# A delta-rule attention followed by two feed-forward layers: weight conversions one step earlier, chunk 1's attention pieces respaced

## The chip, the core and the metric

The kernel runs on one core of a Trainium2 chip. The metric is the device time of one launch in microseconds; the median of three runs is quoted, and one further execution was recorded by the profiler.

## What is computed

With B = 4, H = 8, S = 768, D = 48, all in float32:

```python
k_n = k / (norm(k) + 1e-6)
for t in range(S):                       # per batch and head, state is D x D
    y[t] = q[t] @ state
    v_old = k_n[t] @ state
    state = state + beta[t] * outer(k_n[t], v[t] - v_old)
x = y as [3072 tokens, 384]
x = relu(x @ w_in) ** 2 @ w_out          # 384 -> 2048 -> 384
out = max(x @ w1, x @ w2, x @ w3) @ w3out  # 384 -> 768 -> 384
```

The weights arrive as 64-bit words and are turned into float32 on the chip.

## The kernel before

**Chunks.** The sequence is cut into 12 chunks of 64 tokens. Within a chunk the recurrence becomes a triangular system. Its 64x64 inverse per head is built from two 32x32 inverses and one merging block. The 32x32 inverses of two chunks are computed together by `solve32` on VectorE: a preparation (`prep`, with the norms of the keys), 30 pairs of small operations (lines 290 and 292) and a last product (line 293), whose result goes to DRAM (`finish32`). The products of keys that it starts from, and the masked query-key products, come from `kkps`, which multiplies on TensorE, copies with ACT (line 204), masks with VectorE (line 205) and stores to DRAM from SP.

**Attention of a chunk** (`attention(c)`) is a generator whose pieces are: `load` (`load_x`: the inverses and a key block from DRAM), `st0` (v is scaled; pA and pY = keys and queries times the state Sb; v minus pA), `zz` (pZ, the merging block's first product, with the copy z and the transpose xT), `ww` (pW, written back into xb), `mm_u` (U = inverse times v, in pU; copied by line 480 or 482 to SBUF), `st2` (pY gets the masked products times u, pD the state's growth; Sb is added by line 505, yy copied out by lines 530 and 532) and `st3` (transposes pT, split into xh and xl). Heads go in two groups p = 0 and 1, called pairs below. pA, pZ, pW, pU, pD, pT and the norms' transpose pt share one PSUM tag "at" with two buffers.

U doesn't fit into one bank: units from n on go into spare columns of another bank. Pair 1 uses its own pY for two units (n = 6), pair 0 uses px, the bank of the second product, for four (n = 4); in chunk 2 both use pY.

**The first feed-forward layer of a chunk** (`moe_a`) has 8 products `s1` (18 matmuls of 256 columns into p1, of which there are two buffers; then ACT's Relu, Square and copy gh, and VectorE's gl) and 8 products `s2` (12 matmuls of 384 columns into px), two behind. Every number is split into a high part rounded to the matmul's format and a low part, so each product has three matmuls. At the end px is transposed to xs on VectorE (line 618) and stored.

**The order of the work** is written out by `steps` (line 633). It runs through the steps of `moe_a` of chunk c (16, or 32 halves in chunk 1) and behind each step takes from every other generator as many pieces as are due: a number is a rate per step, a list names the steps. In step order, the generators of `extra` come one after the other. During chunk c the attention of chunk c + 1 runs, and in odd chunks `kkps`, in even chunks the solve for the two chunks behind. Chunk 0 also has `weights`.

The program's order is a priority: a scheduler then places the instructions on each engine by simulated time. From chunk 1 on `pin` (line 263) chains TensorE's and VectorE's instructions, so that these two engines keep the order as written; in chunk 0 nothing is pinned, and ACT, POOL and SP never are. `behind(a, b)` orders a after b.

**Conversions.** A block of w_in or w_out is fetched by SP (line 93) into one of 16 raw buffers, 9 of them for the first blocks only. `turn` (line 101) then takes ACT's magnitude (104), VectorE's shift (107), two joins (111, 113), ACT's high part (115) and VectorE's low part (118). Four of the w_out blocks take two more ACT operations (125, 126) in place of VectorE's. Nine of the 32 blocks are turned ahead of chunk 0; `weights(3, 2)` (line 757) turns three in its first call and two in each of the ten others, and fetches the next. It orders the shifts behind the last but one gl that has been written (`after[:] = gls[-2:-1]`), and the next steps of the solve behind its last low part.

**Norms.** `norm(nm)` transposes the norms on TensorE (pt, line 282) and copies them to normT with four ACT copies (line 318). In `solve32` it is called for all groups but the first at pair 24 of the solve.

**Queues.** `load_x` issues on SP and ACT for chunk 0 and on POOL for all other chunks.

Of the kernel before, what the change touches and what calls it, by code (L numbers as in the profile page):

```python
# [35 lines left out]
HALVED = [(c, c + 1) for c in range(0, NC, 2)]  # L36
U2 = 2 * Q


def delta_moe(ctx, tc, kc, ab, kt, vt, beta, beta32, beta16, kq, w_in, w_out, w1, w2, w3, w_out2, out):  # L40
    nc = tc.nc
    vec, act, pool = nc.vector, nc.scalar, nc.gpsimd
# [151 lines left out]
    def kkps(cs, ps_, dma=nc.sync):  # L194

        todo = [(c, p) for c in cs for p in range(2)]
        ahead = len(kcts) - (len(kcts) < 4)
        for n in range(min(ahead, len(todo))):
            kkp_load(*todo[n], dma)
        for n, (c, p) in enumerate(todo):  # L200
            ks = kss[nk[1] % len(kss)]
            nk[1] += 1
            pk, pq = kk_matmul(c, p, ps_[n % len(ps_)])
            kk_ends[0] = act.copy(ks[:, 0], pk).ins
            kk_ends[1] = vec.tensor_mul(out=ks[:, 1], in0=pq, in1=mask.unsqueeze(1).broadcast_to([128, U2, C])).ins
            for i in mul_after:
                behind(kk_ends[1], i)
            yield
            kk_store(c, p, ks[:, 0], dma)

            for t in range(2):
                dma.dma_start(p_d[c][64 * t:64 * t + 64, U2 * p:U2 * p + U2], ks[64 - 64 * t:128 - 64 * t, 1])
            if n + ahead < len(todo):
                kkp_load(*todo[n + ahead], dma)
            yield
# [122 lines left out]
    def load_x(c):  # L338

        k21 = att.tile([128, B * Q, 32], F32, name="k21", tag="k21", bufs=1)  # L340
        x1 = att.tile([128, U2, 32], F32, name="x1", tag="x1", bufs=1)
        ds = []
        for t in range(2):
            if c:
                ds.append(pool.dma_start(k21[64 * t + 32:64 * t + 64], kk_d[c][32:64, t, :, 0:32]))
            for h in range(2):
                o, hs = 64 * t + 32 * h, slice(32 * h, 32 * h + 32)
                i = (pool if c else (nc.sync, act)[t]).dma_start(xb[o:o + 32, :, hs], xt_d[c][h, t].rearrange("u j i -> j u i"))
                if c:
                    ds.append(i)  # L350
                else:
                    x_loaded.append(i.ins)
        for t in range(2):
            for g in range(2):
                o = 64 * t + 32 * g
                i = (pool if c else (nc.sync, act)[t]).dma_start(x1[o:o + 32], xt_d[c][0, t, U2 * g:U2 * g + U2].rearrange("u j i -> j u i"))
                ds.append(i)
        for i in x_after:
            if c:
                for d in ds:  # L360
                    behind(d.ins, i)
        return k21, x1
# [25 lines left out]
    def attention(c):  # L388
# [68 lines left out]
        def mm_u(p):  # L457
            x, r = tiles[c, p][2], tiles[c, p][6]
            pU = ps_at.tile([128, U2, D], F32, name="pU", tag="at")
            own = p or c == 2  # L460
            n = U2 - (0 if not c else 2 if own else 4)
            if c:
                free = pYs[p] if own else pxs
                over = free[0].rearrange("p (b n) -> p b n", b=1) if own else free[0]
                over = over[:, :, DM:DM + 2 * D].rearrange("p b (u d) -> p b u d", d=D)
            order = [u for i in range(U2) for u in (i, n + i) if (i < n if u == i else u < U2)]
            for u in order:
                for t in range(2):
                    if u < n:
                        pe.matmul(pU[half(t), u], x[half(t), u], r[half(t), u], start=True, stop=True)  # L470
                    else:
                        o = over[half(1 - t), (u - n) // 2, (u - n) % 2]
                        i = pe.matmul(o, x[half(t), u], r[half(t), u], start=False, stop=True, skip_group_check=True)
                        for j in free[1:]:
                            behind(i.ins, j)
            u_ = fresh("u", p, 7, [128, U2, D])
            on_vec = p and c != 1
            def put(to, po):
                if on_vec:
                    last_vec[0] = vec.tensor_copy(to, po).ins  # L480
                else:
                    last_act[0] = act.copy(to, po).ins
            put(u_[:, 0:n], pU[:, 0:n])
            if c:
                for m in range(n, U2, 2):
                    for t in range(2):
                        put(u_[half(t), m:m + 2], over[half(1 - t), (m - n) // 2])
# [214 lines left out]
    def part(g, n):  # L702
        for _ in range(n):
            next(g, None)
            yield
# [5 lines left out]
    if True:  # L711
# [19 lines left out]
        def solve32(g, load=(nc.sync, nc.sync), store=((nc.sync,) * 2,) * 2, landing=0):  # L731
            M, a, ready, norm = start32(g, load)
            for _ in range(landing):
                yield
            if landing:
                prep_after[:] = last_gl
            nm = ready()
            if not g:
                normed.append(norm(nm))
            yield  # L740
            for n, i in enumerate(solve(vec, M, 32, 64 * len(HALVED[g]), a, tmp32)):
                for j in solve_after:
                    behind(i.ins, j)
                ops.append(i.ins)
                if g and n == 24:
                    norm(nm)
                yield
            finish32(g, M, store)

        def later(n, g):  # L750
            for _ in range(n):
                yield
            yield from g
# [3 lines left out]
        def weights(first, each):  # L757
            n = first
            while queue:
                if last_gl[0] and last_gl[0] not in gls:  # L760
                    gls.append(last_gl[0])
                after[:] = gls[-2:-1]
                words(n)
                n = each
                after.clear()
                prep_after[:] = solve_after[:] = parted[-1:]
                yield
# [136 lines left out]
        ahead_ = {}  # L904
        for c in range(NC):
            extra = []
            if c == 0:
                solve_next = solve32(1, (pool,) * 2)
                extra += [(1.0, weights(3, 2)), (11 / 15.0, later(3, attention(1))), (4.0, later(20, part(solve_next, 10)))]
            elif c == 1:  # L910
                pinned.update({first_matmul.ins.engine: None, last_gl[0].engine: None})
                first_solve = [0] * 3 + [1 + n * 13 // 20 for n in range(20)]
                extra += [(first_solve, solve_next), ([14, 16, 24, 25, 27, 29, 31], attention(2))]
                ahead_[2] = solve32(2, landing=1)
                extra += [([13, 14, 18, 19, 20, 21, 22, 23], kkps(HALVED[2], (at,))), ([26], ahead_[2], True)]
                solve_after[:] = last_vec
                prep_after.clear()
            elif c + 1 < NC:
                extra.append(([1, 2, 5 + c // 9, 7 + c // 9, 10, 12, 14] if c % 2 else [1, 2, 4, 6, 8, 11, 13], attention(c + 1)))
            if c == 2:  # L920
                kc_after.clear()
                solve_after.clear()
            if c in ahead_:
                extra.append(([1] * (c == 2) + [1 + (c == 2) + n * (14 - (c == 2)) // 32 for n in range(32)], ahead_[c]))
            if c > 1 and c in KK:
                extra.append(([3, 4, 4, 5, 6, 7, 8, 9], kkps(HALVED[KK[c]], (at,))))
                ahead_[c + 1] = solve32(KK[c], landing=1)
                extra.append(([11, 14], ahead_[c + 1], True))
            if c == 9:
                after[:] = last_gl  # L930
                load_w3s = w3load((0, 1))
            if 9 <= c < NC - 1:
                extra.append((0.4, part(load_w3s, 6)) if c > 9 else (0.8, later(6, part(load_w3s, 6))))
            if c == NC - 1:
                pr.close()
                wb = ctx.enter_context(tc.tile_pool(name="wb", bufs=1, side="right", reuse_waits="tile"))
                first = []
                extra.append((0.6, chain(load_w3s, w3load((2,)))))
                extra.append((0.5, later(2, x2_steps(0, wb, first))))
            steps(moe_a(c, gp, c == 1), *extra)  # L940
# [114 lines left out]
```

## Time and profile before

| | |
|---|---|
| median of 3 runs | 946.04 us (945.61 to 950.18) |
| the profiled execution's own time | 944.06 us |
| its span, first to last instruction | 942.3 us |
| TensorE busy (PE) | 875.7 us, 93% |
| VectorE busy (DVE) | 498.9 us, 53% |
| ACT busy | 391.6 us, 42% |
| GpSimd busy (POOL) | 150.9 us, 16% |
| mean granted TensorE clock | 0.954 of 2.4 GHz |

The profile names an engine's work by line, output and input tile. Busy times are sums over instructions; a busy TensorE isn't one at its peak. Where an engine stood still, the row says for how long and which instruction on which engine ended the wait ("issue": nothing that the profile shows). The granted clock is a share of 2.4 GHz; 0.50 is 1.2 GHz. Chunk 0's first product begins at 76.7 us of the span, chunk 1's at 142.2, chunk 2's at 196.7.

### The profile page before, as it was taken

Reading aid. Unit: us, or ns where it says so; the run is one execution under the profiler, and the core shown is the slowest. Engines: PE = TensorE matmul, PEld = TensorE weight load, DVE = VectorE, ACT = ScalarE, POOL = GpSimd, SP = SyncE. Lnnn points to the kernel's source line nnn. Section 1 sums busy time; section 2 is a strip of 40 time slices with the busy share of each in tenths; the row PEclk is TensorE's granted clock in tenths of the full one; section 3 lists DMA queues with packets and bytes.
Section 4 is the critical chain, followed back from the end, with each engine's and each line's share of the span. In section 5 each row is a group of like instructions: output and inputs, shape, how many; then the busy total and the mean of one; then the engine's idle time right before and its main releaser. Section 6 shows DMA issues by size and latency. Waiting matters only on the chain.

```text
span 942.3 us, 26555 instructions
## 1 busy us (share of the span) xinstructions
PE 875.7 (93%) x11422; PEld 848.9 (90%) x11422; DVE 498.9 (53%) x1118; ACT 391.6 (42%) x807; POOL 150.9 (16%) x245
## 2 busy tenths in 40 slices
PE   4448978998999999999999999999999999999998
PEld 4347868898999999999999999999999999999998
DVE  2987979169427843784388275577432323323221
ACT  1665774334344534453544466564221222212211
POOL 2252110331231124012311420002000000000000
PEclk8557979999999999999999999999999999999999
DMA  9987722762583267327621643234200101000000
GB/s 197 318 226 202 213 75 67 209 149 64 133 193 101 63 146 200 81 63 181 148 61 61 156 126 98 59 106 139 76 22 30 43 26 33 27 26 9 18 17 34
DMA packets 121125, 98.83 MB, mean 105 GB/s; under 512 B 75904, under 2 KB 101296, under 8 KB 121008
## 3 DMA queue, kind: packets, MB, share of 16 engines
q1 hardware_dynamic: 100224, 58.23, 24.3%
q0 software_dynamic: 11712, 32.41, 12.9%
q10 hardware_dynamic: 9072, 6.49, 2.4%
q8 instruction: 90, 1.47, 0.7%
q14 instruction: 27, 0.22, 0.1%
HBM read 72.45 MB, written 24.64 MB: 103 GB/s over the span
## 4 chain that ended last, share of the span: by engine, by line
PE 81%; DVE 7%; ACT 6%; DMA 4%; issue 2%; ACTq 0%; SPq 0%; DVEq 0%
PE p L963 24%; PE px L598 20%; PE p L578 19%; PE po L980 8%; DMA rawp<-in_moe_w_in_dram 2%; PE pU L470 2%; PE pY L520 1%; DVE gl L587 1%; PE pk L187 1%; DVE buf L290 1%; PE pA L451 1%; DVE buf L292 1%; DMA raw<-in_moe_w_out_dram 1%; PE pW L426 1%; PE pZ L417 1%
## 5 line engine op out<-in xcount | busy, mean ns | idle before, releaser
L963 PE MATMUL p<-x_h,w 128*128 128x384 f32 x864 | 220.1, 336 | 0.0
L598 PE MATMUL px<-wout,gh 128*128 128x384 f32 x768 | 204.7, 347 | 1.6 <-ACT wout L115 1.5
L578 PE MATMUL p<-xh,win_h 128*128 128x256 f32 x576 | 169.7, 295 | 2.4 <-DVE gl L587 0.9
L578 PE MATMUL p<-xl,win_h 128*128 128x256 f32 x576 | 163.9, 285 | 0.3 <-DVE xl L542 0.3
L578 PE MATMUL p<-xh,win_l 128*128 128x256 f32 x576 | 164.0, 285 | 0.0
L963 PEld LDWEIGHTS p<-x_h,w 128*128 128x128 f32 x864 | 156.1, 188 | 0.0
L587 DVE TENSOR_TENSOR gl<-p,gh 128x512 fp32r<-128x512 f32 x96 | 66.3, 690 | 154.5 <-ACT gh L586 154.3
L963 PE MATMUL p<-x_l,w 128*128 128x384 f32 x432 | 145.2, 336 | 0.0
L598 PEld LDWEIGHTS px<-wout,gh 128*128 128x128 f32 x768 | 138.7, 194 | 3.2 <-ACT wout L115 1.8
L584 ACT ACTIVATE p<-p 128x512 f32<-128x512 f32 x96 | 55.9, 582 | 187.8 <-PE p L578 186.7
L598 PE MATMUL px<-wout,gl 128*128 128x384 f32 x384 | 131.1, 341 | 0.0
L578 PEld LDWEIGHTS p<-xh,win_h 128*128 128x128 f32 x576 | 111.0, 193 | 6.0 <-DVE gl L587 1.4
L578 PEld LDWEIGHTS p<-xl,win_h 128*128 128x128 f32 x576 | 111.1, 193 | 0.8 <-DVE xl L542 0.7
L578 PEld LDWEIGHTS p<-xh,win_l 128*128 128x128 f32 x576 | 111.3, 193 | 0.0
L969 DVE TENSOR_TENSOR mx<-p,mx 128x384 f32<-128x384 f32 x48 | 26.7, 557 | 124.1 <-PE p L963 124.1
L963 PEld LDWEIGHTS p<-x_l,w 128*128 128x128 f32 x432 | 81.2, 188 | 0.0
L971 ACT CAST hh<-mx 128x384 fp32r<-128x384 f32 x48 | 24.6, 513 | 119.6 <-DVE mx L970 119.5
L598 PEld LDWEIGHTS px<-wout,gl 128*128 128x128 f32 x384 | 74.1, 193 | 0.0
L292 DVE TENSOR_TENSOR buf<-buf 128x30 f32<-128x30 f32 (+9 forms) x180 | 60.5, 336 | 6.0
L290 DVE TENSOR_TENSOR buf<-buf 128x30 f32<-128x30 f32 (+9 forms) x180 | 59.9, 333 | 4.8
L586 ACT CAST gh<-p 128x512 fp32r<-128x512 f32 x96 | 56.4, 588 | 2.5
L585 ACT ACTIVATE p<-p 128x512 f32<-128x512 f32 x96 | 56.0, 583 | 2.6
(183 smaller groups left out, 1341.9 us busy)
## 6 DMA issues: line engine op xcount, KB each, us to landing
kq<-in_kc_dram POOLq DMA_DIRECT2D x22, 448.0 KB, 5.5
raw<-in_moe_w_dram SPq DMA_DIRECT2D x18, 384.0 KB, 3.5
p<-p POOLq DMA_DIRECT2D x22, 256.0 KB, 3.9
raw<-in_moe_w_out_dram SPq DMA_DIRECT2D x13, 384.0 KB, 3.3
v<-in_vt_dram POOLq DMA_DIRECT2D x24, 192.0 KB, 3.4
ktp<-in_kt_dram POOLq DMA_DIRECT2D x24, 192.0 KB, 3.8
x<-xs SPq DMA_DIRECT2D x48, 96.0 KB, 2.7
xr<-x SPq DMA_DIRECT2D x96, 48.0 KB, 1.9
```

The costliest lines, as they stand in the source:

```text
L290: eng.tensor_tensor(out=tv, in0=M[:, 0:j, j].unsqueeze(2).broadcast_to([u, j, m]), in1=M[:, j, j + 1:n].unsqueeze(1).broadcast_to([u, j, m ...
L292: yield eng.tensor_tensor(out=M[:, 0:j, j + 1:n], in0=M[:, 0:j, j + 1:n], in1=tv, op=ALU.add)
L578: pe.matmul(p1[:, j], w[:, k, f], x[c][:, k], start=n == 0 and j == 0, stop=n == 8, skip_group_check=True)
L584: act.activation(out=p1, in_=p1, func=AF.Relu)
L585: act.activation(out=p1, in_=p1, func=AF.Square)
L586: last_gh[0] = act.copy(gh, p1).ins
L587: last_gl[0] = vec.tensor_sub(out=gl, in0=p1, in1=gh.bitcast(F32)).ins
L598: g = pe.matmul(px[:, h, 0:DM], x[:, j, hs], w, start=f == 0 and i == 0, stop=f == NF - 1 and i == 2, skip_group_check=True)
L963: pe.matmul(p, w[i][:, k, fs], x[:, k], start=n == 0, stop=n == 8)
L969: vec.tensor_max(out=t, in0=ps[1], in1=t)
L971: act.copy(hh[:, f], t2)
L980: pe.matmul(po[:, 0:DM], x[:, f, js], w[:, f], start=i == 0, stop=i == 17)
```

## The change

In chunk 0, `weights` is called from step 0 on instead of step 1, and behind the attention's pieces of that step: each call so stands ahead of the step's products that it stood behind before, and its order against the attention's pieces stays. In chunk 1, the pieces of attention(2) and of `kkps` come a step later, except `zz` and `st3`, which stay, and solve32(2)'s preparation moves from step 1 of chunk 2 to the last step of chunk 1; its 32 further pieces are spread over steps 1 to 14 of chunk 2. In `mm_u`, pair 0 of chunk 1 uses its own pY for two units instead of px for four. In `load_x`, chunk 2's inverses of t = 1 (four transfers) are issued by SP instead of POOL. For the solves from the third group on, `norm` is called at pair 8 instead of pair 24, which is step 4 of the even chunk, behind the piece `zz`, instead of step 11, behind `st2`.

```diff
--- before.py
+++ after.py
@@ -340,12 +340,13 @@
         k21 = att.tile([128, B * Q, 32], F32, name="k21", tag="k21", bufs=1)
         x1 = att.tile([128, U2, 32], F32, name="x1", tag="x1", bufs=1)
         ds = []
+        queues = (pool, pool) if c > 2 or c == 1 else (pool, nc.sync) if c else (nc.sync, act)
         for t in range(2):
             if c:
                 ds.append(pool.dma_start(k21[64 * t + 32:64 * t + 64], kk_d[c][32:64, t, :, 0:32]))
             for h in range(2):
                 o, hs = 64 * t + 32 * h, slice(32 * h, 32 * h + 32)
-                i = (pool if c else (nc.sync, act)[t]).dma_start(xb[o:o + 32, :, hs], xt_d[c][h, t].rearrange("u j i -> j u i"))
+                i = queues[t].dma_start(xb[o:o + 32, :, hs], xt_d[c][h, t].rearrange("u j i -> j u i"))
                 if c:
                     ds.append(i)
                 else:
@@ -353,7 +354,7 @@
         for t in range(2):
             for g in range(2):
                 o = 64 * t + 32 * g
-                i = (pool if c else (nc.sync, act)[t]).dma_start(x1[o:o + 32], xt_d[c][0, t, U2 * g:U2 * g + U2].rearrange("u j i -> j u i"))
+                i = queues[t].dma_start(x1[o:o + 32], xt_d[c][0, t, U2 * g:U2 * g + U2].rearrange("u j i -> j u i"))
                 ds.append(i)
         for i in x_after:
             if c:
@@ -457,7 +458,7 @@
         def mm_u(p):
             x, r = tiles[c, p][2], tiles[c, p][6]
             pU = ps_at.tile([128, U2, D], F32, name="pU", tag="at")
-            own = p or c == 2
+            own = p or c <= 2
             n = U2 - (0 if not c else 2 if own else 4)
             if c:
                 free = pYs[p] if own else pxs
@@ -742,7 +743,7 @@
                 for j in solve_after:
                     behind(i.ins, j)
                 ops.append(i.ins)
-                if g and n == 24:
+                if g and n == (24 if g == 1 else 8):
                     norm(nm)
                 yield
             finish32(g, M, store)
@@ -906,13 +907,13 @@
             extra = []
             if c == 0:
                 solve_next = solve32(1, (pool,) * 2)
-                extra += [(1.0, weights(3, 2)), (11 / 15.0, later(3, attention(1))), (4.0, later(20, part(solve_next, 10)))]
+                extra += [(11 / 15.0, later(3, attention(1))), (list(range(17)), weights(3, 2)), (4.0, later(20, part(solve_next, 10)))]
             elif c == 1:
                 pinned.update({first_matmul.ins.engine: None, last_gl[0].engine: None})
                 first_solve = [0] * 3 + [1 + n * 13 // 20 for n in range(20)]
-                extra += [(first_solve, solve_next), ([14, 16, 24, 25, 27, 29, 31], attention(2))]
+                extra += [(first_solve, solve_next), ([15, 17, 24, 26, 28, 30, 31], attention(2))]
                 ahead_[2] = solve32(2, landing=1)
-                extra += [([13, 14, 18, 19, 20, 21, 22, 23], kkps(HALVED[2], (at,))), ([26], ahead_[2], True)]
+                extra += [([14, 15, 19, 20, 21, 22, 23, 24], kkps(HALVED[2], (at,))), ([26, 32], ahead_[2], True)]
                 solve_after[:] = last_vec
                 prep_after.clear()
             elif c + 1 < NC:
@@ -921,7 +922,7 @@
                 kc_after.clear()
                 solve_after.clear()
             if c in ahead_:
-                extra.append(([1] * (c == 2) + [1 + (c == 2) + n * (14 - (c == 2)) // 32 for n in range(32)], ahead_[c]))
+                extra.append(([1 + n * 14 // 32 for n in range(32)], ahead_[c]))
             if c > 1 and c in KK:
                 extra.append(([3, 4, 4, 5, 6, 7, 8, 9], kkps(HALVED[KK[c]], (at,))))
                 ahead_[c + 1] = solve32(KK[c], landing=1)
```

## Rows read from the trace of the kernel before

**Rows 1.** Chunks 0 and 1: length; busy PE, PEld, DVE, ACT, POOL (instructions); clock; DMA share, GB/s.

```profile
76.70:142.00 65.30, 56.27 (x730) 51.81 (x726) 50.90 (x127) 46.80 (x97) 8.14 (x13) 0.84 0.54 154
142.00:201.50 59.50, 55.14 (x998) 51.84 (x1000) 31.98 (x76) 23.80 (x51) 15.60 (x26) 0.97 0.60 149
```

**Rows 2.** What TensorE waited for, whole span: total us, times, longest us.

```profile
PE pt L282 <- DVE Sb L505: 5.8, 4, 2.5
PE pY L520 <- ACT u L482: 5.7, 1, 5.7
...
PE pA L451 <- DVE buf L205: 1.7, 1, 1.7
PE pW L426 <- issue: 1.7, 1, 1.7
PE px L598 <- ACT wout L115: 1.5, 2, 1.0
...
PE pZ L417 <- DVE v L455: 0.9, 1, 0.9
```

**Rows 3.** Two stretches late in chunk 0, columns as in rows 1.

```profile
105.00:125.40 20.40, 17.46 (x338) 15.35 (x337) 16.32 (x44) 18.45 (x39) 3.76 (x5) 0.83 0.58 167
125.40:131.10 5.70, 0.03 (x2) 0.03 (x2) 4.43 (x14) 5.59 (x12) 0.55 (x1) 0.81 0.30 82
```

**Rows 4.** ACT's timeline, 118 to 132 us: start, duration.

```profile
119.65 0.24 ACT L482 COPY u<-pY 64x96 f32<-64x96 f32 x1
...
130.79 0.99 ACT L482 COPY u<-px 64x96 f32<-64x96 f32 x4
```

**Rows 5.** The chain that ended last, in order of time: start, us, what.

```profile
131.83 4.15 PE px L598 x12
136.59 4.40 PE px L598 x24
...
150.25 2.08 PE px L598 x12
...
180.21 0.68 PE pZ L417 x50
...
192.84 2.29 PE px L598 x12
...
231.90 3.46 PE px L598 x12
```

**Rows 6.** ACT's and VectorE's timelines, 72 to 145 us; in brackets, idle time before.

```profile
75.32 1.03 ACT L104 ACTIVATE cvt<-big 128x384 f32<-128x384 f32 x2 [0.31 <-DVE rawp L111]
...
85.48 0.69 DVE L587 TENSOR_TENSOR gl<-p,gh 128x512 fp32r<-128x512 f32 x1 [5.03 <-ACT gh L586]
86.09 0.62 DVE L107 TENSOR_SCALAR cvt<-cvt 128x384 int32<-128x384 int32 x2
...
89.90 1.02 DVE L118 TENSOR_TENSOR wout<-big,wout 128x384 fp32r<-128x384 f32 x2
...
133.23 0.55 DVE L118 TENSOR_TENSOR wout<-raw,wout 128x384 fp32r<-128x384 f32 x1
```

**Rows 7.** VectorE's timeline in chunk 1.

```profile
162.13 0.68 DVE L205 TENSOR_TENSOR buf<-pq,mask 128x512 f32<-128x512 f32 x1
...
193.50 1.46 DVE L530 COPY yy<-pY 64x192 f32<-64x192 f32 x4
```

**Rows 8.** POOL's issues of loads for chunk 2.

```profile
171.14 1.29 POOL L348 DMA_DIRECT2D xb<-xt  x2
```

**Rows 9.** VectorE's timeline, end of chunk 1 and start of chunk 2.

```profile
196.94 1.04 DVE L618 STREAM_TRANSPOSE xs<-px 128x384 f32<-128x384 f32 x2
201.12 0.69 DVE L587 TENSOR_TENSOR gl<-p,gh 128x512 fp32r<-128x512 f32 x1 [3.15 <-ACT gh L586]
...
206.84 0.69 DVE L587 TENSOR_TENSOR gl<-p,gh 128x512 fp32r<-128x512 f32 x1
```

**Rows 10.** TensorE's timeline, first matmul of chunk 0's third product.

```profile
87.08 0.39 PE L578 MATMUL p<-xh,win_h 128*128 128x256 f32 x1
```

## The prediction

> **What bounds the kernel now.** Read the stages first. The stretch of chunk 0 takes 65.3 us with TensorE busy for 56.27 of them at a granted clock of 0.84; chunk 1's 59.5 us have 55.14 at 0.97 [rows 1]. TensorE carries the chain in both, so a microsecond in which it stands still there, or runs at 1.2 GHz in place of 2.4, is a microsecond of the whole. The second view is what TensorE waits for [rows 2]. Of that list the prologue's waits don't concern this change. The rest is one wait of 5.7 us for ACT's copies u (line 482), four for Sb (line 505) in front of the norms' transposes pt (5.8 together, the longest 2.5, so 1.1 in each of the three others), 1.7 for the masked product of line 205, 1.7 marked "issue" in front of pW, 1.5 for converted w_out blocks and 0.9 for v.
>
> Why do the u copies come so late? The windows of chunk 0 show it [rows 3]: from 105.0 to 125.4 us ACT is busy for 18.45 of 20.4 us, and while TensorE stands still (125.4 to 131.1) for 5.59 of 5.7. ACT works through conversions in order; the copies of pair 1's overflow, from pY, run at 119.65, but pair 0's, from px, only at 130.79 [rows 4]. When TensorE resumes, its clock has fallen: twelve products px take 4.15 us from 131.83, where the same twelve take 2.08 at 150.25 [rows 5]. The chunk's last product ends at 136.59 + 4.40 = 141.0 [rows 5].
>
> The early half of the chunk has the room that the late half lacks. VectorE idles 5.03 us before its first gl, at 85.48, and only then takes the shift, joins and lows of two w_out blocks: 0.62 for the pair of shifts and 1.02 for each pair of the three other operations, 3.7 us [rows 6]. Their data had long been there, for ACT took their magnitudes at 75.32 [rows 6]; line 109 orders the shift behind that gl. The last low part of chunk 0 is at 133.23 to 133.8 [rows 6].
>
> **The change, part by part.** All sums are made against the profiled execution's 944.06 us (span 942.3); the median of the runs is 946.04, 1.98 above it, which I add at the end.
>
> Conversions ahead of the products, and the overflow in pY. Each call of weights comes a step earlier, so what its first shift must follow is a gl earlier as well; the first pair of w_out blocks follows none. Nothing is added: the same 23 blocks, the same fetches. They are moved past the Relu, Square, gh and gl of one product on ACT and VectorE, their fetches past nothing on SP but each other, and solve32(1)'s steps come behind one pair more, which is a pair earlier done. The 3.7 us of the first pair now fit into the 5.03 us of idling, and all later blocks, which follow each other through the raw buffers, come about 3.7 us sooner: the last low at 130.1. Pair 0's overflow of chunk 1 moves from px to pY, as pair 1 has it: two copies of 64x96 in place of four, about 0.5 us less for ACT, and they can run beside pair 1's at 119.65, not at 130.79 [rows 4]. Then TensorE goes on at 125.4. What it did from 131.1 to 141.0 is 9.9 us, less 4.15 - 2.08 = 2.1 at the lower clock, 7.8; it would end at 133.2. The words allow 130.1 + 2.1 for the last product = 132.2. The later of both is 133.2: **7.8 us gained**. Bounds: nothing, if the copies are again queued late; 5.1 if the words come no earlier (133.8 + 2.1 = 135.9); 9.3 with the 1.5 us of waits for w_out gone too. I take 7.8, since both its causes have rows of their own; what may stall anew is the second rival.
>
> Chunk 1's pieces, a step later. kkps's first product moves to step 14 and st0 to 15, so half a product stage of px (half of 2.08, 1.04) comes between them. But the mul of line 205 now stands behind a gl (as long as the mul, 0.68) [rows 7]. TensorE's wait becomes 1.7 + 0.7 - 1.0 = 1.4: 0.3 gained, between 0 and the whole 1.7. The solve steps in front of it keep VectorE full, so I stay near the low end. At the end of the chunk st2 and st3 come closer: twelve px products (2.29 from 192.84) lay between st2 and pT, now six (1.1 to 1.2). VectorE's yy, which pT of pair 1 needs, ends at 193.50 + 1.46 = 194.96 [rows 5, 7]. TensorE would be there at 192.84 + 1.15 = 194.0, and does pair 0's pT first: **0.7 lost**, between 0 and 1.0. The 1.7 in front of pW isn't touched.
>
> The inverses of chunk 2 on two queues. Four of POOL's issues, 0.65 each (1.29 for two [rows 8]), go to SP. The last of them are out at 172.4 and pZ starts at 180.21 without a wait [rows 5, 8], so Z doesn't feel it: 0. SP's fetches of keys behind them come at most 2.6 us later and nothing waits for them within that; if that cover were gone, or if Z did wait, it would be 2.6 either way. The Trainium skill (Trainium Kernel Development and Optimization, Key Constraints) speaks against hoping for more: queues on several engines share the same DMA engines, and a second one saves only the sequencer's issue time. By that rule alone the sum would be at best 2.6 us lower; by the row it is unchanged, and the row's start of pZ decides.
>
> solve32(2)'s preparation at the end of chunk 1. On VectorE it fills the time between the end of one gl, 201.8, and the next at 206.84, 5.0 us in which it mostly waits for itself [rows 9]. It moves to behind the transposes xs, which end at 198.0. It still lies in front of chunk 2's first gl, which then comes at 198.0 + 5.0 = 203.0 in place of 201.1, up to 2 us late. Who waits for that is the third product, which takes over its PSUM buffer; a whole product and st0 lie in between, so 0.3 lost (0 to 2.0). Behind it everything on VectorE is up to 5 us earlier, so the 0.9 us wait of pZ for v goes: 0.9 gained.
>
> The norms' transposes behind Z. The transpose itself and its four copies stay, and only their place changes: from right behind st2, where both "at" buffers hold pD until Sb is added, to step 4, right behind pZ, where the pA buffers are free once v is subtracted. That takes away the 2.5 in chunk 2, and the clock's fall behind it (the next twelve px take 3.46, not 2.08 [rows 5]): 3.9. In the three later chunks it is 3 x 1.1 = 3.3, with no fall. What is late next is pT, which waits for yy; yy comes right behind Sb, and two whole product stages (some 4 us at the 2.08 of [rows 5]) lie between. Bounds: 3.3 (if the fall of the clock and half of the wait stay) to 7.2. I take **7.2**.
>
> Sum: -7.8 - 0.3 + 0.7 + 0 + 0.3 - 0.9 - 3.9 - 3.3 = **-15.2**. 944.06 - 15.2 = 928.9, and with the 1.98 to the median **930.8 us**.
>
> **The rivals.** *Only the fixed order gains.* From chunk 1 on TensorE and VectorE keep the order as written; in chunk 0 the scheduler places instructions itself and already put the first three blocks ahead of the first product. If it leaves ACT's queue as full as now, TensorE's wait in chunk 0 only changes its name (px for w_out in place of pY for u). Then 15.2 - 7.8 = 7.4 is left: 938.6. For it speaks ACT's 18.45 of 20.4 us [rows 3], against it the idle 5.03 us. If the norms' transposes then meet another wait too (v's subtraction at Z), half of the 7.2 is gone too and the result, 942.2, is within 0.5% of no change.
>
> *More than counted.* With the waits for w_out (1.5) and for line 205 (another 1.4) gone, and no half clock behind them (about 2), it would be 4.9 less: 925.9.
>
> *Slower: gl behind the words.* Conversions now have precedence over the elementwise work of the product that follows. A gl that stands behind one pair comes 3.7 us late, and the product two further on needs its PSUM buffer: the first gl ends at 86.17 and that product runs at 87.08 [rows 6, 10], so 0.9 us are free. It decides from half a block in front of each gl on. If it hit all eight products at 3.7 - 0.9 = 2.8 us, 22.4 would be lost, 7.4 gained elsewhere: 961. Against it: no gl in chunk 0 has TensorE waiting for it now, and the words' data come one pair at a time.
>
> **How the numbers follow.** My forecast has 0.52, more than counted 0.10, only the fixed order 0.22, next to nothing left 0.10, slower 0.06. The range from 923.5 to 941.0 takes in the first three with their bounds (the terms' best ends, 9.3, 1.7, 2.6, 0.9 and 7.2, and the 2 of the clock make 23.7, or 922.3) and leaves out the last two and a little of the others. This kernel's measurement can tell about 0.5%, 4.7 us, from no change: faster means below 941.3. The first three cases lie there: 0.84; same 0.10; slower 0.06.
>
> **What would show it.** In TensorE's waits the 5.7 us for u and the four waits of pt should be gone, the first stretch should end near 133, and the granted clock between 125 and 142 and between 230 and 240 should be 1.00. VectorE's idle 5 us before the first gl should be filled with shifts and joins. A new wait of pT for yy of some 0.7 us should stand at the end of chunk 1, and line 205's should be little changed. A wait of px for w_out of over 3 us, or of p for gl in chunk 0, would prove the first step wrong.

## The result and the profile after

The changed kernel takes 932.45 us (median; 930.88 to 933.22), the kernel before 947.19 (median of four, the three of 946.04 among them). The ratio is 0.9839 [0.9809, 0.9869], so 1.6% faster; 930.8 was forecast and the range was 923.5 to 941.0. The profiled execution took 932.73 us, its span is 930.8.

The two traces are compared by stages, each from a chunk's first product to the next chunk's: chunk 0, 1, 2 and the rest. These are windows of the kernel before, columns as in [rows 1]:

```profile
76.75:142.25 65.50, 56.22 (x728) 51.81 (x726) 51.10 (x127) 46.97 (x97) 8.14 (x13) 0.84 0.54 154
142.25:196.66 54.41, 50.32 (x952) 47.35 (x952) 30.04 (x72) 21.79 (x46) 15.60 (x26) 0.97 0.61 152
196.66:244.25 47.59, 44.19 (x697) 42.58 (x697) 37.09 (x100) 19.78 (x45) 6.98 (x11) 0.96 0.25 68
244.25:942.30 698.05, 689.71 (x8228) 674.68 (x8227) 328.07 (x699) 266.36 (x555) 90.34 (x143) 1.00 0.32 84
```

and of the changed kernel:

```profile
77.06:136.94 59.88, 53.27 (x728) 48.88 (x726) 51.08 (x126) 47.09 (x95) 8.28 (x13) 0.88 0.61 168
136.94:192.78 55.84, 49.23 (x951) 45.73 (x952) 30.97 (x73) 21.88 (x46) 13.13 (x22) 1.00 0.59 153
192.78:235.58 42.80, 42.41 (x696) 41.01 (x696) 37.57 (x100) 19.86 (x45) 7.01 (x11) 1.00 0.27 70
235.58:930.80 695.22, 689.78 (x8228) 674.82 (x8227) 327.81 (x699) 265.86 (x555) 90.18 (x143) 1.00 0.32 84
```

Chunk 0 is 5.6 us shorter, chunk 1 1.4 longer, chunk 2 4.8 shorter, the rest 2.8, and the start comes 0.3 later: 11.5 us of the span. In chunk 0 TensorE stands still for 2.7 us less (65.50 - 56.22 against 59.88 - 53.27); the other 2.9 us are less busy time for the same 728 matmul records, at a granted clock of 0.88 in place of 0.84. A second profiled execution of the same kernel, r_change below, has the first three stages as

```profile
76.55:135.72 59.17, 52.49 (x728) 48.68 (x727) 51.77 (x127) 47.01 (x95) 9.00 (x13) 0.87 0.60 172
135.72:189.48 53.76, 49.22 (x951) 45.72 (x952) 30.41 (x72) 21.86 (x46) 13.13 (x22) 1.00 0.61 157
189.48:232.29 42.81, 42.41 (x697) 41.01 (x696) 37.58 (x100) 19.84 (x45) 7.00 (x11) 1.00 0.26 72
```

and 14.6 us less span than the kernel before, near the difference of the medians. What differs most between the two is chunk 1, 55.84 and 53.76.

What TensorE waited for, over the whole span, in the changed kernel (the prologue's waits and those that were there unchanged are left out):

```profile
PE pY L521 <- ACT u L483: 3.4, 2, 2.4
PE p L579 <- DVE gl L588: 2.8, 4, 1.5
...
PE pW L427 <- issue: 1.8, 1, 1.8
...
PE pA L452 <- DVE buf L205: 1.1, 1, 1.1
PE p L579 <- DVE xl L543: 0.9, 1, 0.9
...
PE px L599 <- ACT wout L115: 0.2, 1, 0.2
```

Against [rows 2]: the four waits of pt are gone, and so is pZ's for v. The wait for u fell from 5.7 to 3.4 but isn't gone. px waits 0.2 for converted blocks, not 1.5. p waited for gl before too, twice and at most 0.5 us, but never in chunk 0. There a wait for gl is new, the longest of the four, on TensorE's timeline:

```profile
111.94 0.39 PE L579 MATMUL p<-xh,win_h 128*128 128x256 f32 x1 [1.50 <-DVE gl L588]
```

The copies of u run on ACT so:

```profile
123.89 0.48 ACT L483 COPY u<-pY 64x96 f32<-64x96 f32 x2
...
127.16 0.48 ACT L483 COPY u<-pY 64x96 f32<-64x96 f32 x2
127.66 0.40 ACT L483 COPY u<-pU 128x288 f32<-128x288 f32 x1
```

Both pairs' copies come between 123.9 and 128.1, not beside 119.65 [rows 4]. Two things upstream of them have moved. ACT copies pW into xb, which U's products need, 3.3 us later; the kernel before, then the changed one:

```profile
115.11 1.51 ACT L433 COPY xb<-pW 32x256 f32<-32x256 f32 x4
```

```profile
118.38 1.62 ACT L434 COPY xb<-pW 32x256 f32<-32x256 f32 x4
```

So U's first product runs at 118.89 us, not at 115.51. And in the kernel before it was not ACT alone that kept pair 0's overflow: TensorE multiplied it into px only here, some 7 us behind pair 1's, and ACT copied it some 6 us after that:

```profile
123.75 0.49 PE L473 MATMUL px<-v,xb 64*64 64x48 f32 x10
```

Between 105.0 and 125.4 us ACT is still busy for 17.93 us, where it was 18.45 [rows 3]; what has changed in that stretch is the clock, 1.00 in place of 0.83:

```profile
105.00:125.40 20.40, 15.35 (x265) 13.08 (x265) 16.83 (x42) 17.93 (x37) 3.77 (x5) 1.00 0.55 155
```

The fall behind the wait for u is still there. From 125 to 142 us the clock is 0.80 in both kernels (before, then after):

```profile
125.00:142.00 17.00, 10.87 (x97) 9.88 (x88) 12.66 (x37) 10.85 (x27) 2.47 (x5) 0.80 0.22 67
```

```profile
125.00:142.00 17.00, 14.26 (x191) 13.53 (x192) 14.97 (x41) 9.28 (x23) 2.17 (x4) 0.80 0.30 78
```

Read in slices of 1 us, it is at 0.50 from 129 to 135 before, and from 126 to 132 in the changed kernel and in r_change. Two other stretches at 0.50 in the kernel before, 109 to 111 and 119 to 122, aren't in the changed kernel's trace; r_change has one, 112 to 115, behind its wait for gl.

VectorE's first gl and the last low part of chunk 0, the two rows that answer to [rows 6]:

```profile
85.79 0.69 DVE L588 TENSOR_TENSOR gl<-p,gh 128x512 fp32r<-128x512 f32 x1 [2.64 <-ACT gh L587]
```

```profile
130.92 0.56 DVE L118 TENSOR_TENSOR wout<-raw,wout 128x384 fp32r<-128x384 f32 x1
```

The idle time before the first gl fell from 5.03 to 2.64 us, and the words end at 131.5, not 133.8: 2.3 us sooner, where 3.7 was counted. In r_change they end at 129.4, 4.4 us sooner.

In chunk 1, SP issues its share of chunk 2's inverses and then the keys for `kkps` (SPq is SP's queue of transfers), and TensorE's product of keys waits for those:

```profile
161.83 1.91 SPq L349 DMA_DIRECT2D xb<-xt  x2
...
165.96 0.40 SPq L174 DMA_DIRECT2D big<-in_kc_dram  x1
```

```profile
172.86 0.27 PE L187 MATMUL pk<-big 48*64 48x64 f32 x2 [1.69 <-DMA big<-in_kc_dram]
```

At the end of the chunk pT waits for yy as worked out (0.7):

```profile
191.37 0.52 PE L539 MATMUL pT<-ident,yy 128*128 128x128 f32 x3 [0.70 <-DVE yy L531]
```

### The profile page after: what moved, and what is told of

The parts are those of the page before. It is cut to its first block, busy times and chain, and to the rows that moved or that the text cites. A ratio compares the mean times of both kernels' runs of the same rounds, so it can differ in the third digit from the quotient of the medians.

```text
span 930.8 us, 26555 instructions
## 1 busy us (share of the span) xinstructions
PE 869.7 (93%) x11422; PEld 842.8 (91%) x11422; DVE 499.8 (54%) x1118; ACT 391.3 (42%) x805; POOL 148.2 (16%) x241
## 4 chain that ended last, share of the span: by engine, by line
PE 77%; DVE 9%; DMA 7%; ACT 4%; issue 2%; POOL 1%; SPq 0%; ACTq 0%; DVEq 0%; POOLq 0%
PE p L964 24%; PE px L599 18%; PE p L579 18%; PE po L981 8%; DVE buf L290 2%; DVE buf L292 2%; PE pY L521 2%; PE pU L471 2%; DMA xt<-buf 1%; DVE gl L588 1%; PE pk L187 1%; DMA kct<-in_kc_dram 1%; DMA raw<-in_moe_w_in_dram 1%; PE pW L427 1%; PE pZ L418 1%
## 5 line engine op out<-in xcount | busy, mean ns | idle before, releaser
L599 PE MATMUL px<-wout,gh 128*128 128x384 f32 x768 | 201.0, 342 | 0.3 <-ACT wout L115 0.2
L599 PEld LDWEIGHTS px<-wout,gh 128*128 128x128 f32 x768 | 135.2, 189 | 2.4 <-ACT wout L115 0.5
L599 PE MATMUL px<-wout,gl 128*128 128x384 f32 x384 | 129.1, 336 | 0.0
```

The costliest lines, as they stand in the source:

```text
L599: g = pe.matmul(px[:, h, 0:DM], x[:, j, hs], w, start=f == 0 and i == 0, stop=f == NF - 1 and i == 2, skip_group_check=True)
```

## The experiments

The table gives for each run the median, its ratio to the kernel before, measured beside it, and from its trace the stages from first product to first product. The stages are windows as above.

| run | us | ratio [95%] | span | chunk 0 | chunk 1 | chunk 2 |
|---|---|---|---|---|---|---|
| before | | | 942.3 | 65.50 | 54.41 | 47.59 |
| the change | 932.45 | 0.9839 [0.9809, 0.9869] | 930.8 | 59.88 | 55.84 | 42.80 |
| r_change, once more | 930.63 | 0.9845 [0.9823, 0.9867] | 927.7 | 59.17 | 53.76 | 42.81 |
| u_weights | 934.42 | 0.9896 [0.9866, 0.9927] | 932.7 | 60.34 | 58.06 | 42.81 |
| u_px | 931.53 | 0.9864 [0.9836, 0.9892] | 930.0 | 58.51 | 56.30 | 42.80 |
| o_px | 939.17 | 0.9955 [0.9933, 0.9977] | 939.2 | 58.75 | 57.68 | 47.65 |
| o_weights | 937.85 | 0.9948 [0.9924, 0.9973] | 936.4 | 58.40 | 54.83 | 46.10 |
| u_norm | 936.18 | 0.9917 [0.9889, 0.9946] | 934.9 | 58.75 | 55.80 | 43.95 |
| o_norm | 938.71 | 0.9947 [0.9928, 0.9966] | 937.9 | 63.84 | 57.36 | 43.59 |
| u_prep | 932.88 | 0.9887 [0.9866, 0.9907] | 928.3 | 57.87 | 56.06 | 43.47 |
| u_pool | 930.67 | 0.9865 [0.9835, 0.9895] | 927.3 | 58.69 | 53.43 | 42.80 |
| n_pool_st2 | 929.87 | 0.9839 [0.9817, 0.9861] | 926.9 | 57.68 | 55.34 | 42.92 |
| n_vec | 931.48 | 0.9849 [0.9826, 0.9872] | 929.9 | 57.99 | 56.12 | 45.46 |
| n_words | 931.59 | 0.9857 [0.9833, 0.9882] | 929.9 | 56.21 | 56.16 | 43.96 |

The kernel before had medians of 947.19 us beside the change, 943.33 beside the runs u_weights, u_px, u_norm and u_pool, 943.69 beside u_prep and the o runs, and 945.27 beside r_change and the n runs; so times from different groups are compared by their ratios. Ratios tell apart some 0.3 to 0.5%; within that, the stages have to do it, and a stage too differs between executions: chunk 0 of the kernel before took 65.50 us, and 63.84 in o_norm, where nothing in it is changed.

### Chunk 0: the place of the conversions, or the overflow?

**u_weights** takes the first part of the change back:

```diff
-extra += [(11 / 15.0, later(3, attention(1))), (list(range(17)), weights(3, 2)), ...
+extra += [(1.0, weights(3, 2)), (11 / 15.0, later(3, attention(1))), ...
```

> The change with chunk 0's conversions put back behind each step's products. Theory: the conversions' new place and the overflow in pY share chunk 0's gain; without the first the words come some 2.3 us later (last low part near 133.8, as before) and the last product waits for them: 2 to 3 us slower than the change, about 935. Rival A, the overflow in pY did it all: within 0.7 us of the change, and no idle VectorE is needed. Rival B, the new place did it all: chunk 0 ends near 141.6 again, 5 to 6 us slower, 938.

Measured: 934.42 us. Chunk 0 takes 60.3 us, little more than with the change (59.2 and 59.9), and there is no wait for u in it. What is lost is lost in chunk 1, 58.1 us, where the other five runs with SP's loads took 53.8 to 56.3. These are TensorE's two longest waits there:

```profile
PE pk L187 <- DMA big<-in_kc_dram: 2.2, 1, 2.2
PE p L579 <- DVE gl L588: 2.0, 1, 2.0
```

The last product of chunk 0 now runs after pT; behind it come the transposes xs and then gl on VectorE, in the order as written, and the third product of chunk 1 waits 2.0 us for its buffer. The time is some 3 us above u_px and u_pool (931.53 and 930.67 beside it), within the intervals; the size is as the theory has it (2 to 3 us), the place isn't. ACT's copies of u run at 116.8 to 120.1 us here, as early as the prediction had them.

**u_px** takes the second part back instead (`own = p or c == 2`).

> The change with pair 0's overflow of chunk 1 back in px (four units, four small copies). Theory: its copies are queued late on ACT again, and TensorE's waits for u in chunk 0 grow from 3.4 us by 1.5 to 3: 934 to 936. Rival, the conversions' new place alone cured the queue: the waits stay near 3.4 and the time within 0.7 us of the change. If both this and the run with the conversions put back lose little, either alone suffices.

Measured: 931.53 us; chunk 0 takes 58.5 us. TensorE's longest wait in it:

```profile
PE pY L521 <- ACT u L483: 2.3, 1, 2.3
```

The wait for u is 2.3 us, less than the change's 3.4 (behind it come gl and xb with 1.6 each). The rival holds: with the conversions ahead, the overflow's place adds nothing that can be seen.

**o_px** and **o_weights** make the same two edits one at a time in the kernel before.

> The kernel before with one part alone: pair 0's overflow of chunk 1 in pY. Theory: either this or the conversions' new place suffices for nearly all of chunk 0's gain. The stretch from chunk 0's first product to the end of pT falls from 64.9 to about 59 us, the 5.7 us wait for u goes and waits for converted blocks take over part of it; the rest of the kernel is as before: some 6 us faster than before, 0.6%. Rival, the prediction's: with the words as late as before the stretch ends at 5.1 us less at best, and if the copies stay late on ACT nothing is gained.

> The kernel before with one part alone: chunk 0's conversions ahead of each step's products, the overflow still in px. Theory: the stretch falls from 64.9 to 58 to 59 us as with both, waits for u of 2 to 3 us stay, a wait for the first layer's gl of 1.5 to 2 is new: some 6 us faster than before. Rival: the px copies come after the conversions on ACT in any order, and the 5.7 us stay: chunk 0 gains at most 2 us.

Measured: o_px 939.17 us with 58.75 for chunk 0, o_weights 937.85 with 58.40. TensorE's longest waits in chunk 0 of o_px:

```profile
PE px L598 <- ACT wout L133: 2.5, 1, 2.5
PE px L598 <- ACT wout L115: 1.6, 2, 1.0
PE p L578 <- ACT win_h L115: 0.8, 1, 0.8
```

In chunk 1 of it p waits 2.0 us for gl, as in u_weights; here too chunk 0's last product runs after pT. The copies of u run as early as in u_weights, the first of them here:

```profile
116.78 0.48 ACT L482 COPY u<-pY 64x96 f32<-64x96 f32 x2
```

TensorE's longest waits in chunk 0 of o_weights:

```profile
PE pY L520 <- ACT u L482: 2.3, 1, 2.3
PE p L578 <- DVE gl L587: 2.1, 1, 2.1
PE pU L470 <- ACT xb L433: 1.4, 1, 1.4
```

So each edit alone cuts chunk 0 from 65.5 us by 6.8 or 7.1 (from o_norm's 63.84 by 5.1 or 5.4), and both together by about as much (5.6 to 7.8, or 4.0 to 6.2, in the six runs that have both and change nothing else there). With the overflow alone, waits for words of 5.3 us (2.3 of them were there before) take the place of the 5.7 for u; TensorE's waits in the chunk still add up to 5.6 us instead of 8.3, and the mean clock is 0.90 instead of 0.84. With the conversions alone the wait for u is 2.3, gl and xb take up a part with 3.5 together, and the sum is 6.8. With both it is 5.9, and 6.1 in r_change. The two edits work against each other: counted from chunk 0's first product, ACT's copies of pW start at 36.1 to 38.4 us in the four runs without the conversions' move and at 38.7 to 41.3 in the ten with it. U follows them, and the copies of u, early in o_px and u_weights, are late again.

The theory had 0.6% for each; measured are 0.45 and 0.52%, which the intervals neither tell apart nor tell from 0.6. In the traces chunk 1 is 3.3 us longer than before in o_px and 0.4 in o_weights. Of o_px's 3.3 no more than the wait for gl can be put down to the edit: o_norm, whose first two chunks are those of the kernel before, has 57.36 there, 3.0 longer.

### Chunk 2: the norms' transposes, or the preparation?

**u_norm** sets the transposes back (`if g and n == 24`), **o_norm** makes that edit alone in the kernel before (`24 if g == 1 else 8`), **u_prep** sets the preparation back to step 1 of chunk 2 (`[26]`, and 33 pieces in chunk 2).

> The change with the norms' transposes back at pair 24, right behind st2. Theory: the three waits of 1.1 us in the later chunks are back, and in chunk 2, where VectorE is no longer late since the preparation left, one of 1.1 too without a fall of the clock: 4.4 us slower than the change, about 937. Rival, the prediction's own price: 2.5 and 1.4 for the clock in chunk 2 and 3.3 later, 7.2 us slower, 939.6, if the preparation's move does not matter to them.

> The kernel before with one part alone: the norms' transposes of the later groups at pair 8, behind Z. Theory: 1.1 us in each of three later chunks and, in chunk 2, nearly all of the 2.5 and of the clock's 1.4, though VectorE is still late there, for the next product does not wait for Sb: 6 to 7 us faster than before; Z's wait of 0.9 stays. Rival: the preparation's move is what cured chunk 2. VectorE is late, pt behind Z waits for the subtraction of v and pT later for yy: chunk 2 keeps 2 us or more of waits, and only 4 to 5 us are gained in all.

> The change with solve32(2)'s preparation back at step 1 of chunk 2. Theory: the norms' transposes are out of the way, so only Z's wait of 0.9 for v returns, pt behind it adds up to 0.4, and the 0.4 in front of the third product goes: chunk 2 takes 43.5 to 44 us, not 42.8: about 1 us slower than the change. Rival: VectorE's lateness costs more, pT waits for yy and the clock falls at it: chunk 2 near 46, 3 us slower.

Measured for u_norm: 936.18 us; four waits of 1.1 are back and the clock doesn't fall:

```profile
PE pt L282 <- DVE Sb L506: 4.3, 4, 1.1
```

Chunk 2 and the rest of the span in u_norm, then in o_norm, then chunk 2 in u_prep:

```profile
192.19:236.14 43.95, 42.47 (x696) 41.01 (x696) 37.59 (x100) 19.97 (x45) 7.02 (x11) 1.00 0.25 70
236.14:934.90 698.76, 690.16 (x8228) 674.89 (x8227) 327.93 (x699) 266.49 (x555) 90.00 (x143) 1.00 0.31 83
```

```profile
198.87:242.46 43.59, 42.71 (x696) 41.16 (x696) 36.94 (x100) 19.59 (x45) 6.96 (x11) 1.00 0.25 67
242.46:937.90 695.44, 689.80 (x8228) 674.78 (x8227) 327.98 (x700) 265.99 (x555) 90.08 (x143) 1.00 0.31 84
```

```profile
190.66:234.13 43.47, 42.59 (x696) 41.17 (x696) 36.89 (x100) 19.59 (x45) 6.96 (x11) 1.00 0.25 69
```

In u_norm chunk 2 is 1.15 us longer than with the change and the rest 3.5, 4.7 together where 4.4 was expected and the prediction's own price was 7.2; by the medians it is 4.7 to 5.5 us slower than u_px and u_pool beside it. In o_norm chunk 2 is 4.0 us shorter than before and the rest 2.6: 6.6, as expected. In u_prep chunk 2 takes 43.47, 0.7 more than with the change (expected 43.5 to 44). So chunk 2's 4.8 us also have two cures of which either brings most: the transposes alone 4.0, the preparation alone 47.59 - 43.95 = 3.6. Some 1.5 us of each is the clock, and that isn't a fixed price of the wait: o_weights, which changes nothing in chunk 2, has the same waits there (2.5 for Sb, 0.9 for v), yet a clock of 1.00 and 46.10 us, where the kernel before and o_px have 0.96 and 47.6. u_prep's ratio, 0.9887 [0.9866, 0.9907], is worse than its trace; the intervals don't settle whether it is more than a microsecond.

### Chunk 1: two queues, and st2 a step later

**u_pool** sets all of chunk 2's inverses back to POOL. **r_change** is the change itself once more.

> The change with all of chunk 2's inverses on POOL again. Theory: the new wait of 1.7 us for the keys of kkps in chunk 1 comes from SP, whose fetch stands behind the four loads that wait for the inverses' stores to land; without them it is gone, Z still doesn't wait, and the kernel is 1.7 us faster than the change, about 930.8. Rival: the loads, now a step later, make Z wait on one queue by 1 us or more, so nothing is won or up to 1 us lost; the wait for keys may stay, if the shifted kkps makes it.

> The change itself once more, beside the three below. All theories expect what it measured: about 15 us under the kernel before, the stretch of chunk 0 near 59 us, the waits for u and for the keys of kkps as before.

Measured: u_pool 930.67 us and r_change 930.63. In u_pool TensorE doesn't wait for keys nor for the inverses, and chunk 1 takes 53.43 us. But in r_change, with SP's loads, the same wait is 0.5 us, and chunk 1 takes 53.76. Over all runs the wait stands in four of the six that issue the loads on SP (1.7, 0.5, 2.2, 0.5 us; none of that name in u_px and u_prep) and in none of the eight that issue them on POOL. So SP's loads make it, as the theory has it, but how long it is differs from execution to execution, and no gain from removing it can be measured. The theory's way to it, a key fetch that stands behind the loads, is a small part: counted from chunk 1's first product SP issues it at 29.0 us in the changed kernel and 28.3 in r_change, 28.1 in u_pool and 28.9 in the kernel before. It is the transfer that takes longer, 6.8 and 5.8 us from issue to landing, against 4.0 and 4.1. Whether it waits behind the loads on the same queue or shares the DMA engines with them isn't shown.

**n_pool_st2** is u_pool with U and st2 of attention(2) a step earlier, as before:

```diff
-[15, 17, 24, 26, 28, 30, 31], attention(2)
+[15, 17, 24, 26, 27, 29, 31], attention(2)
```

> The change with chunk 2's inverses on POOL and st2 and U of attention(2) back a step (27, 29). Theory: the wait of 1.7 us for keys and that of 0.7 for yy at the end of chunk 1 are both gone, chunk 1 takes some 2.4 us less: 2 to 2.5 us faster than the change. Rival: they only hide other waits (line 205's product, the fetch of instructions in front of pW), and less than 1 us is left.

Measured: 929.87 us against r_change's 930.63 beside it: no difference that can be told. The waits for keys and for yy are both gone. Chunk 1:

```profile
133.34:188.68 55.34, 50.55 (x951) 46.96 (x952) 30.34 (x72) 21.81 (x46) 15.60 (x26) 0.97 0.58 156
```

Chunk 1 takes 55.34 us all the same. pW's wait "issue" is 2.2 there, where the change had 1.8 and 1.5, and the clock is at 0.97 where the change had 1.00: 55.34 x 0.03 = 1.7 us. The rival is nearer; that pW's wait is a fetch of instructions, as it has it, no run shows.

### Is ACT the limit of chunk 0?

Two more on top of n_pool_st2: **n_vec** puts pair 1's copies of u in chunk 1 on VectorE (`on_vec = p`), **n_words** leaves block 14 of w_out to VectorE's joins (`if f in (8, 10, 12)`).

> The run before, and pair 1's copies of u in chunk 1 on VectorE, as in the other chunks. Theory: ACT's queue bounds chunk 0's late half, 9.8 of 10 us busy; three copies, 0.9 us, and their place in that queue go to an engine with 2 us free, and the waits for u fall from 3.4 to 2 or less: another 1 to 1.5 us faster. Rival: VectorE works through the words' joins in order too, the copies wait there as long, and the time is the same within 0.7 us or worse.

> The run with POOL and st2, and one w_out block fewer (14) whose sign and joins ACT takes over: 2.1 us of ACT in chunk 0 become 0.7 us more on VectorE. Theory, ACT bounds chunk 0's late half: the last copies of u and the last words come 1 to 2 us sooner, chunk 0 ends 1 to 1.5 us sooner. Rival: both engines are in each other's way, the last low part needs VectorE, and it ends within 0.7 us of the run without.

Measured: n_vec 931.48, n_words 931.59, n_pool_st2 929.87 beside them; nothing gained. In n_vec, TensorE's longest waits in chunk 0:

```profile
PE pY L521 <- ACT u L483: 2.4, 1, 2.4
PE p L579 <- DVE gl L588: 2.1, 1, 2.1
PE pT L539 <- DVE Sb L506: 1.0, 1, 1.0
```

The wait for u falls from n_pool_st2's 4.0 to 2.4, and those for gl and Sb, VectorE's work, come up by 3.1. In n_words:

```profile
78.14:134.35 56.21, 50.70 (x728) 46.61 (x726) 49.41 (x123) 45.27 (x93) 8.33 (x13) 0.92 0.63 179
```

```profile
PE p L579 <- DVE xl L543: 2.8, 1, 2.8
```

Chunk 0 is 1.5 us shorter than in n_pool_st2, as ACT's theory says, though executions of one and the same chunk 0 differ by up to 2.2; then the first product of chunk 1 waits 2.8 us for xl on VectorE (0.5 in n_pool_st2). Both runs also wait 1.4 us for gl in chunk 2 (0.4 in the change), which takes 45.46 and 43.96 us. In these two traces work taken from ACT comes back as a wait for VectorE. No version ran clearly faster than the change.

## Why the prediction was right, and where not

The total was right and so were most signs: the sum was 15.2 us, the medians differ by 14.7. The spans of the two executions of the change are 11.5 and 14.6 us under that of the kernel before, so by the traces the sum was 0.6 to 3.7 too large.

- *Conversions and overflow, 7.8.* Measured 5.6 and 6.3, so the size is near; the way to it is not the predicted one, and the sign that was to prove this step wrong, a wait of p for gl in chunk 0, is there. The step that failed is "they can run beside pair 1's at 119.65". It holds for the overflow alone (116.8 to 120.1 in o_px and u_weights), but with the conversions moved ahead ACT's copies of pW, and so U itself, come some 3 us later, and the copies of both pairs ran at 123.9 to 128.1; TensorE still stood still for u for 3.4 us (4.0 in r_change) of the 5.7. With that wait its fall of the clock stayed, which had been counted as 2.1 gained: the clock from 125 to 142 us is 0.80, as before, not 1.00. In their place came gains that the sum had in its upper bound at most: two other stretches at half clock, of some 3 us each, went (r_change has one of its own, behind gl), and the waits for converted blocks, 2.3 with win_h's, fell to 0.2 or nothing. That the term came out near its size is in part luck. The words came 2.3 us sooner in one execution and 4.4 in the other, against 3.7 counted; VectorE's idle time before the first gl was half filled. I counted two causes as one sum; the runs with one edit each show that either brings most or all of it in chunk 0. With the overflow alone, in o_px and u_weights, chunk 1 then waits 2.0 us for gl.
- *The slower rival, gl behind the words,* is real in small: one wait in chunk 0, of 1.5 us and 2.1 in the two executions, not eight of 2.8. The argument against it, that no gl had TensorE waiting before, didn't carry over.
- *Line 205's wait, 0.3 gained:* it went from 1.7 to 1.1, so 0.6, and the clock stayed at 1.00 in both executions of the change where it was 0.97 before. That second part, some 1.6 us, I had left in the bounds. It isn't shown to come from this wait: seven other runs have the same 1.1 and a clock of 0.97.
- *yy, 0.7 lost:* 0.70, and gone in n_pool_st2, while u_pool still has it: st2's later place was the cause.
- *Two queues, 0.* The bound was 2.6 either way, and "nothing waits for them within that" was wrong: the keys of `kkps` did, by 1.7 and 0.5 us. The rule of the Trainium skill that I set beside it (Trainium Kernel Development and Optimization, Key Constraints), that a second queue saves only issue time, isn't contradicted: Z gained nothing, though it had no wait to lose. What the runs add is a cost on the queue that takes the loads over: its next fetch took 4.9 to 7.6 us to land in the five of these runs in which the trace shows it, and 3.8 to 4.1 with POOL.
- *The preparation, 0.9 gained and 0.3 lost:* pZ's wait is gone, and the third product of chunk 2 waits 0.4 us for gl.
- *The transposes, 3.9 + 3.3.* Chunk 2 is 4.8 us shorter, against 3.9 + 0.9 - 0.3 = 4.5; the rest of the span 2.8 and 2.6. The sum was right, its division not: without the transposes' move the preparation alone would have brought 3.6 of chunk 2's 4.8. And the 1.4 in the 3.9 for the clock's fall was there in two of three executions with the wait of 2.5 (kernel before, o_px), not in o_weights.

By stages, chunk 0 brought 1.5 to 2.2 us less than counted, chunk 1 cost 1.0 more in one execution and 1.1 less in the other, and chunk 2 and the rest together 0.2 and 0.4 less than counted. Of the other signs, the four waits of pt are gone, the clock from 230 to 240 us is 1.00 (0.83 before) and pT's 0.7 for yy is there; chunk 0's last product ends at 135.7 and 134.5 us, not near 133.

## What to carry to other kernels

Where two edits aim at one wait, price them together and ask what each does to the other: here either of two cured most of chunk 0, either of two most of chunk 2, and in chunk 0 the one made the other's copies late again. Where two engines are nearly full, a wait that is cured comes back in part as another: 5.7 us for u became 5.3 for words, or 2.3 for u and 3.5 for gl and xb. So add up what the engine waits for in the stage, and read its clock there, before and after; the one wait's end says little. And moving a load to another queue can cost the next fetch there, so look at that too, not only at who wants the load.

## What was not expected

- The same kernel's chunk 1 took 55.84 and 53.76 us in two executions, 1.2 us of the difference in the one wait for keys; and chunk 0 took 57.7 to 59.9 us over six runs in which nothing differed there. The kernel before varies more: beside the u runs it took 940.1 us in an execution with a mean clock of 0.962 and 947.9 in one with 0.951.
- In chunk 1 the granted clock was 1.00 over the whole stage in some runs and 0.97 in others (0.94 in o_px and o_norm), 1.6 us per fall, with waits of the same names and nearly the same lengths. What decided it stays open.
- pW's wait "issue" in chunk 1 was between 0.4 us (n_words) and 3.1 (o_norm), though none of the edits names it. It lies within pW's 64 matmuls: 58 of them ran ahead of it in the kernel before, 50 in the changed one.
